# Causal mask of a segment-recurrent attention: a mask product on TensorE replaced by a minimum on VectorE, with a new order of operations

## The chip, the cores and the metric

The kernel runs on one core of a Trainium2 chip. The core has five engines that the text names as the profile does: PE (TensorE, matrix products into the accumulation banks; PEld are its weight loads), DVE (VectorE), ACT (ScalarE), POOL (GpSimd) and SP (SyncE, which issues most DMAs). Each engine works through its own instruction list in the written order and waits on semaphores of the others. The metric is device time in microseconds of one launch, lower is better. A profile is one further execution, taken by the hardware profiler.

## The reference, cut to what matters

Two attention branches read the same `x` (2048 rows of 512, bfloat16) and are mixed by a gate per row. Branch A is the one that the change touches. It goes through the rows in 64 segments of 32 rows, with 8 memory rows in front of each:

```python
mask = (idx[:, None] < M) | (idx[:, None] >= idx[None, :])   # M = 8, idx = 0..39
for s in range(n_seg):                                        # 64 segments
    h = jnp.concatenate([mem, xs], axis=1)                    # 8 memory rows + 32 rows
    q, k, v = h @ Wq, h @ Wk, h @ Wv                          # 32 heads of 128
    scores = where(mask, q k^T * scale, -1e9)
    o = softmax(scores) v, then Wo
    mem = o[:, :M]                                            # the next segment needs this
    outs.append(o[:, M:])
return g * a + (1 - g) * b
```

So segment s + 1 cannot project its memory rows before segment s has been through all of it. Memory rows see every column; the others see columns up to their own. Branch B is a causal softmax attention in four blocks of 512 rows with a small memory between the blocks; its parts hang less on each other.

## The kernel before, in words

**Work.** A class `Prog` records every operation with its engine, its reads and its writes. `ORDER`, a packed text at the head of the file, then says for each engine in which order the operations stand; semaphores are put in from the reads and writes. Where an operation may run on either of two engines (the copies out of the accumulation banks on ACT or DVE, some small products on DVE or POOL), `ORDER` decides that too. So the engines are in order, and what stands behind a waiting instruction waits with it.

**A segment** (`p_seg`) treats 24 of its rows and the 8 memory rows as keys and columns of `hT`; the last 8 rows of every segment don't depend on the memory as keys, and their projections come from batches for four segments at once (`p_rest`, tiles `xr`, `rem_k`, `rem_q`, `rem_v`). The steps are, for each half of the heads (r = 0 and 1, 16 heads each):

- projections of K and Q (line 1422, `Wk_sb,hT` and `Wq_sb,hT`, 16 matrix products each of 512 columns, or two times 16 of 256 columns for the last Q), copied to `st` by ACT or DVE (line 1002) and transposed on DVE into `KT_sb` and `QT_sb` (line 1497);
- the mask product (operation `H`, `f_hide`, in the profile under the helper's line 1029 with the tiles `hide_sb,neg_sb`): four matrix products of 160 columns that put -1e9 where a score is to be hidden and 0 elsewhere;
- the scores (operation `S`, lines 1512 and 1516), added onto that;
- the exponential on ACT (line 1521) into `PT_sb`, 56 columns for each of four head groups;
- the sums over keys by a product with ones (operation `U`, line 1536), the logarithm of the sums and the exponential of its negative on ACT (lines 1540 and 1542: the reciprocal), and the products with it on DVE and POOL (lines 1544 and 1546);
- the values (operations `PV` and `PW`, lines 1577 and 1586), copied to `OT_sb`.

After both halves comes the output projection (line 1314, `Wo_sb,OT_sb`, 64 matrix products), a transposition on DVE (line 1332), the exchange of two halves (line 1335) and the sum that writes the memory columns of the next `hT` (line 1337). The V projections (line 1422, `Wv_sb,hT`), the batches of `p_rest`, the last rows' output projections (`Wo_sb,OTr_sb`) and all of branch B stand in between as other work.

The lines of the operations that the change touches:

Of the kernel before, what the change touches and what calls it, by code (L numbers as in the profile page):

```python
# [15 lines left out]
    "c-nPZ2|yIp8~@(U?#`aDpc0BE%HfgsomYk;kY(l-rCDN{VwqNIYMyCore%1Rnn!rynSz9h;(Z%lq-kEEsR;@!3(U@&|9i8?yczhf!tTy|^S$r*eZTK}Pd5Y_F;`It7Qt!M>jdXFZ"  # L16
    "o}-UlLQEyp%Znl@BL;{n;K2$&H>mTz4SFmT->}>Uj3k}Ax1#@|F)jy%a)CuJat}R+mVI0VSn<{jtTiAHr)-JHnVW?7+7^4Mjwxk0EEq7O){4P{F=1({YSvLVSQH!nLG4W_PiTg50"
    "2~?Cjevt%qpGqX9JTf2%N|n43{DSW=?CJH`$aW^l;(b7AT27at_>WV<G2E+e=NC_xT4})(%_O;1cK|@!%sMuR5FrosV`z$GZL-ngj8W-QHDeyQR&AmT>-AJX~r9w&EP<vf>k13>}"
    "YuMGWGzU!~8%&JQ-1f(c4LLI~N5IeQV0#?OF2!QE<RZ?L2efGsfP4iSf(uCn}cIN$12`{P+6F9gn+{LDZu1y+Cn%`e0KXaOQp5~=dwr?T)a2rjn0i#RdRP*D_60^lgLUW?-3T5AD"
    "jybi^^oj}%>U%zo>Jb8OZ<N}L1(=#JDDoS_`pkgh2B0%=U>r|~rbo`cqusO2TW~0a<WCe1=<RUh>xlYGAT@awnt*sMpDAF5er(SIgaCr*VEC!Gp!1GiZ{)5^AJm?7j_+?@1XVC66"  # L20
    "fK}v0dtnjOMt8&ES#TM#+-5CV24f)gF^mT=dd2_h7_tMPi`R}>Q*C+|IKc{F8M+b*CahBw{|@l86F&Jw<gJA$VEhbw5jb2flMdk9=>lxN@wK9KSIXHo05@sWTy_w|B0V@xG|X$k!"
    "5Qc(z>l4d0gO{L*8zySK|+AI=Yc|?i|A>-rv~5b&x$60G`~bF5g;`*UeUgp8#$P~WuO<H3;HrU6qp@?poi!G*1ZFJdo>Z@TR5FXf;4NkN4_;Q_>=tEN6g`@fLb1bpaQZOiBXA>+V"
    "H_fUo0j7tZRV`qWIE%l9QVe4i}WBen=dJJ$-3R$`vD)ECd(}i!6v}wbKMbU|KIybFj0I<yVs21`WWjcz74CIxX<zN6}V_>`=sknfI7Lom-iDQqlY4j3tj35S_u#NIL8@#(|@(^gD"
    "q0MO1`W<fvwgK|q|<WpWYQIAZErNVb+NA!hN)%6Z)m)oCLd#K2<P`G#<>Spirme1+>R!DTrEufjoS2e3LBmW(FSix)!Cv_)X{<k$nW+{BAwE4V<Gi@XNJ6qu-J|I%D~`W1pX(dr6"
    "(Zsdy$M1J#|UcaIjK_A87OP!BGmm~3{MiDW2`b1JS#zG4zYL8z&jn!$w&VgMtAR!PCfvr_vXm#I&D5^58Xr!WX?sD?;Wsu1EGvETU^t@Rm^QJ;WnomV`C2^nywC;mQ$Yfy?Ur|D_"
    "+x^7LIRr4fPb(%|7#Kycye@;J*805BKVblW2D^Y*GHwNd0uQboqwdro;&<wLP(!K-hDODb5;6!@=<%CuNDROMkMxyQ!@7G&;`g2uwoqyYIK2&-U4g}V{#iBP3SzT(=$yDIx0r};d"
    "Nfrr`}5L`NyOOQqQPFs*-F9YE_D=Av!#v~1t^1;Pt@?xMDN{1dK?MP(&QfgfDlfp4L48({ACl!_Z={bdSQl?kBP9gHeF!YDiZ}!fSaJ`F@)>OoG{{7l9QCr;5++xqT}nYJ(f%ef~"
    "c~)u+~#VO0>bU0*1m<2xW-kOk04bH`epzFFYc_HvHD-Ka11iv=>z?H<I=tQX?Qxb~61n`atq8hKl#IxN?r?i*2q4HEG5LAY^gk%flVv+w|Ack1N&eV+-P*$I%~$fqC(V=2F6+_tK"
    "`$8cX!18sAl7csb{#;Jk*=Paxt!Za1~P%cZhXN^zu1U15uA4^8D0gNtMmY~^4ON{QNWB&IM|jnZ6*Xhn-kCz4tQhr7rk=C+VQPuR<@C=B(ynW-%49~@;K9!UNyT@S$JF#tytozt5"
    "C5q%x@h_(LpPy`V@*Acw6w7TY-iq_!{C<tnj^Sg(%r<~diL6o##{=@EL37^jN263L+F9ox%n6xg^Gt&DDu=FUTEBz%LVBu$V;StF#Po6I_Sl#@!P^<e$H^}ZKKyE(N>>^7aeuavs"  # L30
    "k{{#SP{$7ig0u5Y#H#>}Wt<&{zDiRhT?0mtAHBEmPeKPL;WPxrHfu(gCf6ag`T(LL?1@J_fS6ROGaBXcH@L-8_<H^ipOtaX;r-0nFvbWeghvU(DST1;KExcXR$dh9w3HG@%d90<&"
    "ZW<b$c$)3=>3m_l&*Y%8{2^}?JvWB^OX~U;fkSdIUfR$4m;v2B`Bx%y#9>54MH3xB7MT$<H0T`m}T6&coXW6Tz;aqV#X!tpSC9S7t)}gBN}W{riGy>zgB*<TzR7uy-}OUuQyyO)-"
    "siOn$h@AL#ivGJ0EhjT1YoyYvW@MFLY>wp|);&Ib8AT;<D}gmu1TFWeRi2Xv>GoU=hpKt%IM&zyT+LjSMg{%J4pXZF;3H(_mrLFQqV+Mk!eItZb1NzWE}MK`K&_YyvM`A%AvKzYV"
    "6M0H<G6fTl+~AFZw|9zwo$KKdS=2?!i51O%%Fm0IS_mN~K|<SP-X20y3A9NgotFGgo9z#&ED)b^)HyWPWZdZABn)#r-7Kv>_;>|+c47YjIdg`vPoNGMcK=SH8l(t6$@=uwE7Cp>8"
    "J4G5f9fY3Gsdp_1c|2}SxF2o#+IoO!z`7&Dd$OV5rg4fas^_$65>v`>`tO75lLm)1OSd4-&iXHX_h^bH?qYv@SS-tpTj8@=i{0!Fx@dx;B>^y*$&Ibf2aaey?M-8ZvZ+2K906G;w"
    "WHuyZ#$|TBj5~wi3Yz~Vw*NjLKy;YPcpls)v}Wj_Jww``O8;rn?AhSbTfj}M4%p7)QNd<#1yT{P@4!jC%?t&m@28UsI&1?}pF;uNPRSB&F4OJ+^+iK~Symw&j*0|(Ke%>FY#=)BN"
    "0spfp&%?Kz=B6z9)ysf+03461+@^^-o}?i&M^U}c-C+77cFah+fy~TfT9r3H41Qh_k%GH?u0wY8qIIZc3Da0hh!jwt)LdMEzr%qwFd=0Yf$sPLpEI?83~L)1Ja1Ir4Am7O(Z5i7H"
    "sQrz;oYifr9W2n9Nw<l2@YM>RO+vTNqYiL!3<xQL)MTck{vq0&;jvo<Gh^0@8rGT41v2z;L1?*n+3d2;pr7mOweE(dIlIws*&e8XG)n-JF5!io%L><BK7Hv&ktcHjy~mb#d?~jV!"
    "hHj}G5V!QGw)64V9AOABTQzYPI(_@{P9>#MSPW`ymLx8jZ+ez)#j6d+sV=8A(zM$#eqPWZlF9-{?1D%y77{uvWcu*Wk2=1nIHIxroS<Q3gq^AiCitVL6|%S*}&loDNz?@|#Ovrg7"
    "tVs-B{y-BQ})dBi8M82qy(AlnBfoa~TlvstPHxaIbt8p>sJ>DE0b{9e41Ft?THB#-==UG!__3IXK+mmE1QP(Vx{pH-D1WKNm@Fcc2U4-G+QC{ppooCOXH7RU|H$SZ$i`v6)H=-7b"  # L40
    "VYu9TE#oa2e;Z&jsaRW&V{)EovUA||DA8f|LP&=Ln{Y%?&x_<KQD;2W0SBf{m_LaM<h6(5pzs2C2JQ12AqAhbglp-*#);na7n|lyhXr4N4HEHLgWwPD#SSD!HVDR{8{Tu6y*US{T"
    "kwLx);kMarJ>-i{{Z3k#8<PtesK_jfMBE~8$sYcJX(AOU-e^=7McSr$ZHXiS};|I!wb9Pdqj^{>_L5m!wW)1Ls6Lb%H0O&)dMxW-~+*eaNMm3PL2ezgRlUCx~tOTlSM@YAZOAy(+"
    "z^dU-Z??&t7;^!!dagxF)QSuheG>mt@P{{&6k&yP1Anj1uhzysfLXqOsecGwI$Kd#-IvuRHeD@OQnTYhdUyFp@WD)?z{RsFYnxlhNo;lcTNY6C1fJ96$HrHx0|rXq`8t&3>?OYX?"
    "<)v4CH<205=bz9qa^@ie%`w2z&>@rdipAA1>}Y<sNaEnKu|7!KOjkIQ_`aOA`+2z);0%UvJ+8~U&==D!`yqx>Z^gP?-f8^WGLRxBJYiwogJsIWS%SPX(jZ_m)f`L?y(R5c1SxjAF"
    "em3A((TYd)g<DKgO4K}3}ggy+(tB<TAIIyr_ivBEgIMqG7`|tZV8~Nw9D~(7yxX?66;Pox<=z@QIw_#p%1sPj_sQLbL4t`I7jDfJ_Z8&ptNO=pV37awgBQ*N`wG}1~GOjj$hb(@x"
    "$L$wMgZv5_=6w(3`p8ws<7k`RxA?wD+K|&itkvnWA-iuO*&o67enCHF?^!q*%58Z1OtOy7fU|ejn+1Dczju7PY33VEZbgYEJY~*<8jquiU0IN@um83IuqEc;fV9~lbWf`VqK&)Wm"
    "@~|T_g<pj2L%-x!C1<pcE^eLHa#6l!5o)a|8f)IZe0_I*B$SjT>DXlfrGOT6Un`zj+c|WkZq92lVI-X?FktNt3M_87S^#sd~n-hT=Dtxk;_RShz%LNchAa`N5NyA-ii47OK#CbjE"
    "4Rc^wok2GbtuAle8~)ID=&y0*D2I*$(JxvpV<c=QYQ<4LMV6CJM-jDZSOqaN@tjO^FD;T4yG=+*XVo7hj_Jsxx99+TA-Oq<sF@XIoYD%>=UYnHDCl>A8##$O79wD6U_|6HbL$lY)"
    "S+undQd2qO6_jog+ZyNH7X6Sog?C!dI=2Pkl1KD5Wikt?t`I+f<+{ntJs*MsKn${?xgeze#OBK1p$Y84|uV=_#Ue~D%h>OFlQU_Ey*&XzU+-hz>jXE^Uix-A&Fr=~#1b49^Jh$ZB"
    "Kj3fJ@+zZ6kmx~U+wPRvFpyWP1U{ofqun~D`&-jOX!<z3!3Fz{j=<AVtzRDBfac~gS&et0pZaR>l_PUYFY0QSs{%Y$07~WG4=}=;-Nj8(vvuTS#-)wPnpQZHPiQHq>dsF0v*66`$"  # L50
    "81>sk!f}o4=bK;Vih@c{_TEkYK(+s%9xsqdfk*h>+efG&@G)9Cb3sM|ByQTA7#@gc%@N^J;~-8?#`T0Lo%$1vTLwZs&QgZSQ{RpY`Y6R#VSYEYZqj_YZflnF*tB*qiP>jM1v76Lx"
    "E0K`Z#2O-8y9gratC7)%HIur>2P_oH=a5yYQkI;n?VCiEI!?xR{q1S1Ny>01x@Z%OiXc3SV99w9Ex1ok02W&F&$f`osM!Wg6KOHpZqKX7=?>w%-6eOCfSAKok<17?w1P)`fgwR$O"
    "OidduJj~x$o(-yYpW(YG}hZ1SQBsGeG8i?(EC<)WH$&EZ#B^F0=#KIRvhU+i`mD-JdS&pVnU<ev@8sI$U`0Hu3RNGCp5lw!B>5^PH|(F4V5>B1tBS4tKQUb5GF4xmyy)en0m6C^L"
# [83 lines left out]
class Slot(Res):  # L137
# [9 lines left out]
    @property  # L147
    def b(self):
        return self.banks[0]
# [1498 lines left out]
```

## Time and profile before

| | |
|---|---|
| time, median of 3 runs | 824.7 us (823.15 to 830.68) |
| the profiled execution: its own time, its span | 824.12 us, 822.2 us |
| PE busy | 795.5 us (97%) |
| PEld busy | 506.2 us (62%) |
| DVE busy | 642.5 us (78%) |
| ACT busy | 523.4 us (64%) |
| POOL busy | 259.7 us (32%) |
| mask products (line 1029, `hide_sb,neg_sb`) | 512, 31.5 us busy, 233 ns mean |
| exponentials (line 1521) | 128, 45.5 us busy, 356 ns mean |
| products with the reciprocal (line 1544) | 128, 44.2 us busy, 345 ns mean |

Span is the time from the first to the last instruction, and the launch's own time is 1.9 us more. Busy times are shares of the span on each engine. Matrix products overlap each other in PE, so the mean duration of one is longer than the time between the starts of two; the busy time is that of their union.

### The profile page before, as it was taken

How to read it: one execution, taken by the hardware profiler on the slowest of the kernel's cores; microseconds unless marked ns; L12 is line 12 of the kernel's file. 1: busy time of each engine (PE TensorE's matmuls, PEld its weight loads, DVE VectorE, ACT ScalarE, POOL GpSimd, SP SyncE). 2: the span in 40 equal slices, each digit the busy share in tenths (PEclk: the TensorE clock that was granted, in tenths of full speed). 3: DMA queues.
4: the chain of work that ended last, by engine and by line, in shares of the span. 5: the costliest groups of instructions: out<-in, count | busy, mean ns of one | idle time of the engine just before them, and what ended most of it. 6: DMA issues, size and time to landing. Idle time of an engine off the chain costs nothing.

```text
span 822.2 us, 51771 instructions
## 1 busy us (share of the span) xinstructions
PE 795.5 (97%) x23607; PEld 506.2 (62%) x23607; DVE 642.5 (78%) x1681; ACT 523.4 (64%) x1198; POOL 259.7 (32%) x564
## 2 busy tenths in 40 slices
PE   9999999999999999999999999999999999999987
PEld 4456666656666566666656665656765666666655
DVE  4878888778879777777877887787876788787886
ACT  4666656776656656767667666577666656766662
POOL 4543221233223332422422322333323223332440
PEclk9999999999999999999999999999999999999999
DMA  9982202121210111121011111100111010010001
GB/s 337 414 243 58 51 9 43 35 51 27 47 25 21 45 27 39 32 46 33 16 37 47 37 24 44 30 24 19 40 47 29 22 30 22 16 25 22 22 21 36
DMA packets 71696, 45.14 MB, mean 55 GB/s; under 512 B 50046, under 2 KB 69942, under 8 KB 69942
## 3 DMA queue, kind: packets, MB, share of 16 engines
q1 hardware_dynamic: 70422, 40.92, 17.6%
q8 instruction: 185, 3.03, 1.6%
q10 hardware_dynamic: 1056, 0.92, 0.4%
q14 instruction: 33, 0.27, 0.1%
HBM read 30.33 MB, written 8.87 MB: 48 GB/s over the span
## 4 chain that ended last, share of the span: by engine, by line
PE 84%; DVE 7%; ACT 3%; DMA 2%; issue 2%; POOL 0%; SPq 0%; DVEq 0%; POOLq 0%
PE pb L1422 45%; PE pb L1314 17%; PE pb L1029 6%; PE pb L1146 4%; PE pb L1577 2%; PE pb L1187 2%; PE pb L1031 2%; PE pb L1512 2%; PE pb L1536 1%; PE pb L790 1%; DMA out_dram<-stg 1%; PE pb L1586 1%; DVE V_sb L1002 1%; PE pb L1235 1%; DVE OT_sb L1002 1%
## 5 line engine op out<-in xcount | busy, mean ns | idle before, releaser
L1164 ACT ACTIVATE PTB<-pb 128x640 bf16<-128x640 f32 x240 | 158.4, 704 | 41.8 <-PE pb L1146 30.5
L1002 ACT ACTIVATE st<-pb 128x512 bf16<-128x512 f32 (+2 forms) x232 | 113.1, 499 | 106.8 <-PE pb L1422 80.7
L1422 PE MATMUL pb<-Wv_sb,hT 128*32 128x512 bf16 x2048 | 153.4, 380 | 0.0
L1422 PE MATMUL pb<-Wq_sb,hT 128*32 128x256 bf16 (+1 forms) x3072 | 140.0, 308 | 0.5 <-DVE hT L1337 0.3
L1314 PE MATMUL pb<-Wo_sb,OT_sb 128*32 128x256 bf16 x4096 | 131.4, 273 | 5.1 <-issue 3.8
L1422 PE MATMUL pb<-Wk_sb,hT 128*32 128x512 bf16 x2048 | 132.3, 379 | 1.0 <-issue 0.6
L1314 PEld LDWEIGHTS pb<-Wo_sb,OT_sb 128*32 128x32 bf16 x4096 | 102.1, 96 | 16.1 <-issue 4.2
L1170 POOL TENSOR_SCALAR_AFFINE_SELECT PTB<-PTB 128x512 bf16<-128x512 bf16 x120 | 78.1, 651 | 90.9 <-ACT PTB L1164 84.3
L1422 PEld LDWEIGHTS pb<-Wq_sb,hT 128*32 128x32 bf16 x3072 | 80.9, 97 | 41.7 <-DVE hT L1337 3.8
L1546 POOL TENSOR_TENSOR PT_sb<-PT_sb,rc_sb 128x64 bf16<-128x64 bf16 x81 | 29.6, 365 | 188.4 <-ACT rc_sb L1542 179.3
L1422 PEld LDWEIGHTS pb<-Wk_sb,hT 128*32 128x32 bf16 x2048 | 54.6, 97 | 48.9 <-DVE ao L1345 2.2
L1002 ACT ACTIVATE OT_sb<-pb 128x320 bf16<-128x320 f32 (+1 forms) x139 | 57.4, 429 | 34.4 <-PE pb L1586 32.2
L1002 DVE CAST st<-pb 128x512 bf16<-128x512 f32 (+1 forms) x123 | 67.2, 549 | 15.4 <-PE pb L1422 12.8
L1002 DVE CAST OT_sb<-pb 128x320 bf16<-128x320 f32 (+2 forms) x121 | 56.5, 475 | 20.6 <-PE pb L1586 18.2
L1002 DVE CAST V_sb<-pb 128x512 bf16<-128x512 f32 x90 | 61.5, 683 | 9.9 <-PE pb L1422 8.8
L1497 DVE STREAM_TRANSPOSE QT_sb<-st 128x128 f32<-128x128 f32 (+1 forms) x192 | 61.8, 334 | 7.8 <-ACT st L1002 5.7
L1540 ACT ACTIVATE rc_sb<-pb 128x160 f32<-128x160 f32 x128 | 38.9, 304 | 43.8 <-PE pb L1536 37.0
L1332 DVE STREAM_TRANSPOSE pb<-pb 128x256 f32<-128x256 f32 x63 | 29.3, 465 | 42.4 <-PE pb L1314 42.2
L1422 PEld LDWEIGHTS pb<-Wv_sb,hT 128*32 128x32 bf16 x2048 | 49.5, 97 | 19.2 <-ACT st L1002 0.7
L1521 ACT ACTIVATE PT_sb<-pb 128x224 bf16<-128x224 f32 x128 | 45.5, 356 | 23.3 <-PE pb L1516 19.4
L1497 DVE STREAM_TRANSPOSE KT_sb<-st 128x256 f32<-128x256 f32 x128 | 54.5, 426 | 7.0 <-ACT st L1002 5.5
L1544 DVE TENSOR_TENSOR PT_sb<-PT_sb,rc_sb 128x160 bf16<-128x160 bf16 x128 | 44.2, 345 | 9.0 <-ACT rc_sb L1542 7.4
(200 smaller groups left out, 1461.3 us busy)
## 6 DMA issues: line engine op xcount, KB each, us to landing
Wv_sb<-in_A_Wv_dram SPq DMA_DIRECT2D x4, 1024.0 KB, 10.1
Wk_sb<-in_A_Wk_dram SPq DMA_DIRECT2D x4, 1024.0 KB, 20.5
Wq_sb<-in_A_Wq_dram SPq DMA_DIRECT2D x4, 1024.0 KB, 27.3
Wo_sb<-in_A_Wo_dram SPq DMA_DIRECT2D x4, 1024.0 KB, 20.7
rest_v<-stg SPq DMA_DIRECT2D x112, 32.0 KB
rem_v<-rest_v SPq DMA_DIRECT2D x28, 128.0 KB, 2.4
a_rows<-ao SPq DMA_DIRECT2D x63, 32.0 KB
stg<-a_rows SPq DMA_DIRECT2D x15, 128.0 KB
```

Source lines behind the costliest of these rows:

```text
L1002: self.P.op(("act", "dve"), (lambda a: a.activation(dst, src(), ACT.Copy), lambda d: d.tensor_copy(dst, src())), reads=reads, writes=write ...
L1029: ins = pe.matmul(out[32 * c:32 * c + 32], lhsT[:, 32 * c:32 * c + 32], rhs, start=start, stop=stop, tile_position=(0, 32 * c), **kw)
L1146: ins = pe.matmul(pb[slot.banks[i]][:, base + a - lo:base + b - lo], KT[r0:r1, 128 * kc:128 * kc + 128], Q[r0:r1, t0 + a:t0 + b], start=Tr ...
L1164: P.op("act", (lambda dst=dst, src=src: lambda a: a.activation(dst, src(), ACT.Exp, scale=0.25))(), reads=[pair], writes=["%s%d_%d" % (nam ...
L1170: P.op("gp", (lambda pt=pt, ii=ii: (lambda g: g.affine_select(pt, pt, ([[0, len(ii)]] if len(ii) > 1 else []) + [[1, 128]], ALU.is_ge, 0.0 ...
L1314: ins = pe.matmul(pb[so.b][p0:p0 + 32, 0:256], tok(r, g, l), half(h, d, q), start=(r == 0 and g == 0 and l < 2), stop=(r == 1 and g == 3 a ...
L1422: ins = pe.matmul(self.pb[sl.b][32 * g:32 * g + 32, 0:hi - lo], x[:, c, 0:32], cols, start=(c == 0), stop=(c == C - 1), tile_position=(0, ...
L1497: op("dve", (lambda dst=dst, src=src: lambda d: d.transpose(dst, src))(), reads=["st%d%s" % (i, tag)], writes=["%sT%d%s" % (kind, r, tag)] ...
L1521: op("act", lambda a: a.activation(PT[:, r, :], pb[rb.b][:, 0:224], ACT.Exp, scale=SCALE), reads=[rb], writes=["PT%d" % r, "PT%dr" % r], n ...
L1540: op("act", lambda a: a.activation(rc[:, r, :], pb[rb.b][:, 0:160], ACT.Ln), reads=[rb], writes=[rr], name="ln%d_%d" % (s, r), cost=t_act( ...
L1544: op("dve", lambda d: d.tensor_tensor(mine[r], mine[r], by_head(rc[:, r, :]), ALU.mult), reads=[rp, rr], writes=[rp], name="nrm%d_%d" % (s ...
L1546: op(("dve", "gp"), tuple((lambda e: e.tensor_tensor(rest[r], rest[r], late(rc[:, r, :]), ALU.mult)) for _ in range(2)), reads=[rp + "r", rr],
```

## The change

The mask product `H` is taken out of each half segment, and the first score product of each group now starts the bank afresh (`start=(l == 0)`). The exponential then works on scores that are not masked. Behind it DVE takes, in place, the minimum of the first 40 columns of each head group of `PT_sb` and a table: zero where the score is to be hidden, 3e38 elsewhere. The sums and the products read `PT_sb` behind that minimum. The table is made once: the old mask product is done a single time (`keep`), and a DVE instruction turns what it gives into zeros and 3e38 and writes it over `hide_sb`. `ORDER` is another text throughout.

```diff
 ORDER = (
-    "c-nPZ2|yIp8~@(U?#`aDpc0BE%HfgsomYk;kY(l-...
+    "c-nPZ2VfLM7k;yQm)&b=1f&NDgx-tvDumudT2Pww...
 )
...
+        sm = P.slot("F")
+        op("pe", lambda pe, m: self.mm(pe, m, pb[sm.b][:, 0:160], self.neg[:, :], self.hide[:, :], True, True), reads=["neg", "hide"], writes=[sm],
+           name="keep", cost=0.08, prio=-0.98, mode=FLEX)
+        op("dve", lambda d: d.tensor_scalar(self.hide[:, :], pb[sm.b][:, 0:160], -0.5, 3e38, op0=ALU.is_ge, op1=ALU.mult), reads=[sm], writes=["hide"],
+           name="keepev", cost=0.3, prio=-0.98)
...
         def p_s(r, i, prio):
             rb = bank()
 
-            def f_hide(pe, m):
-                return self.mm(pe, m, by_head(pb[rb.b][:, 0:224])[:, :, 0:40], self.neg[:, :], self.hide[:, :].rearrange("p (h q) -> p h q", h=4), True, True, skip_group_check=True)
-            op("pe", f_hide, reads=["neg", "hide", "st%d" % i], writes=[rb], name="H%d_%d" % (s, r), cost=0.072, prio=prio, mode=FLEX)
-
             def f_sc(pe):
...
-                                        start=False, stop=True, tile_position=(0, 32 * g), skip_group_check=True)
+                                        start=(l == 0), stop=True, tile_position=(0, 32 * g), skip_group_check=True)
...
             op("act", lambda a: a.activation(PT[:, r, :], pb[rb.b][:, 0:224], ACT.Exp, scale=SCALE), reads=[rb], writes=["PT%d" % r, "PT%dr" % r],
                name="exp%d_%d" % (s, r), cost=t_act(224), prio=prio)
+            op("dve", lambda d: d.tensor_tensor(by_head(PT[:, r, :])[:, :, 0:40], by_head(PT[:, r, :])[:, :, 0:40], by_head(self.hide[:, :]), ALU.min),
+               reads=["hide"], writes=["PT%d" % r, "PT%dr" % r], name="cut%d_%d" % (s, r), cost=0.3, prio=prio)
```

Counted from the two orders: PE issues 505 matrix products fewer (the 512 mask products go; the table's product and other splits of the same work add 7). DVE gets the 128 minima and the table's instruction. Of the copies out of the banks that either engine can make, 39 more stand on ACT than before, counted with the exchanges of line 1335; of the copies of projected K, V and Q alone it is 21, 18 and 24. PE changes between its ways of dividing its array 376 times, before 380 times. The table is made before the first segment's scores.

More of the change, by code (lines that the diff above doesn't have):

```diff
@@ L20 @@
[L20 to L43, printed above, removed]
@@ L76 @@
[L76 to L79 removed]
+    "c-nPZ2VfLM7k;yQm)&b=1f&NDgx-tvDumudT2Pwwj{F296zK>8p-77;9YI7CLI^!-q=q68>7b|-NlY%>C3m+o|IA+5axrk1yV*ByUin@ds9f>|hr{`NKn8ea#0$9j3%O4m2G1%EJ"
@@ L80 @@
+    "J|ox^o^gFnYKX<8oSi@<ct8x0gO0_eq|W+x&Y}apZ*?Mm5;o4uaeg&26xfnh7{;4Q1)s-6c7>Jm6ZP$RW%~(=4RhFqzVsp-5{EVGw=@=Ky;T#N&^>A7X8O%CqddSl@OyF%hyKOH{"
+    "Kx3VfL9*as%)2UF~?u*o~OPC>cFRu)+>eOCsem+j}lO05M3Yp#cWUlE(q#dM}UYZXYl2KX~}>-03d%S3Qn1IjGm@ab6%$ZXR_bKqa69X~5zfrh%losn>+2S12zC0wqErLK?UDViD"
+    "<Xll~8w$TxZ"
 )
```

100 lines of the change are left out of this document (60 added, 40 removed).

## The prediction

> **What bounds the kernel now.** I read the page's busy times first, then the chain that ended last, then one segment in order of time, then who waited for whom on PE's weight loads.
>
> ```profile
> span 822.2 us, 51771 instructions
> PE 795.5 (97%) x23607; PEld 506.2 (62%) x23607; DVE 642.5 (78%) x1681; ACT 523.4 (64%) x1198; POOL 259.7 (32%) x564
> ...
> PE 84%; DVE 7%; ACT 3%; DMA 2%; issue 2%; POOL 0%; SPq 0%; DVEq 0%; POOLq 0%
> ```
>
> By these rows PE is nearly always at work, and any matrix product taken away would be time won. The order of time of one segment, from the memory columns of one to those of the next, tells another story.
>
> ```profile
> 400.37 0.19 DVE L1337 TENSOR_TENSOR hT<-pb,other_sb 128x32 bf16<-128x32 f32 x1
> 400.87 1.04 PE L1422 MATMUL pb<-Wk_sb,hT 128*32 128x512 bf16 x16
> 401.73 1.04 PE L1422 MATMUL pb<-Wq_sb,hT 128*32 128x512 bf16 x16
> 402.14 1.28 ACT L1002 ACTIVATE st<-pb 128x512 bf16<-128x512 f32 x2
> ...
> 403.69 0.40 DVE L1497 STREAM_TRANSPOSE QT_sb<-st 128x256 f32<-128x256 f32 x1
> ...
> 403.68 0.24 PE L1029 MATMUL pb<-hide_sb,neg_sb 128*32 128x160 bf16 x4
> 403.75 0.61 PE L1422 MATMUL pb<-Wq_sb,hT 128*32 128x256 bf16 x16
> 404.40 0.27 PE L1512 MATMUL pb<-QT_sb,KT_sb 128*32 128x40 bf16 x16
> 404.82 0.36 ACT L1521 ACTIVATE PT_sb<-pb 128x224 bf16<-128x224 f32 x1 [1.40 <-PE pb L1516]
> 405.40 0.27 PE L1536 MATMUL pb<-PT_sb,ones_sb 128*32 128x160 bf16 x8
> 405.54 0.49 DVE L1497 STREAM_TRANSPOSE QT_sb<-st 128x128 f32<-128x128 f32 x2
> 406.20 0.25 PE L1029 MATMUL pb<-hide_sb,neg_sb 128*32 128x160 bf16 x4
> 406.27 0.28 PE L1512 MATMUL pb<-QT_sb,KT_sb 128*32 128x40 bf16 x16
> 406.69 0.36 ACT L1521 ACTIVATE PT_sb<-pb 128x224 bf16<-128x224 f32 x1 [0.27 <-PE pb L1516]
> 407.27 0.29 PE L1536 MATMUL pb<-PT_sb,ones_sb 128*32 128x160 bf16 x8
> 407.95 0.34 ACT L1542 ACTIVATE rc_sb<-rc_sb 128x160 f32<-128x160 f32 x1
> 408.32 0.33 DVE L1544 TENSOR_TENSOR PT_sb<-PT_sb,rc_sb 128x160 bf16<-128x160 bf16 x1
> 409.39 0.27 PE L1577 MATMUL pb<-PT_sb,V_sb 32*128 32x40 bf16 x16
> 409.62 1.93 PE L1314 MATMUL pb<-Wo_sb,OT_sb 128*32 128x256 bf16 x64
> 411.61 0.47 DVE L1332 STREAM_TRANSPOSE pb<-pb 128x256 f32<-128x256 f32 x1 [0.82 <-PE pb L1314]
> 412.55 0.19 DVE L1337 TENSOR_TENSOR hT<-pb,other_sb 128x32 bf16<-128x32 f32 x1 [0.26 <-ACT other_sb L1335]
> ```
>
> From 400.37 to 412.55 are 12.18 us, and 64 such turns are 780 us of the 822.2. So the time is that of this ring of steps, and PE's other work is laid into it in a written order. The reader is to see two kinds of links. In the tight ones the next engine starts as soon as it can: the product with the reciprocal starts at 408.32, 0.03 us behind the reciprocal's end (407.95 and 0.34), the turn at 411.61 right behind the output projection. In the slack ones PE is late, because other work stands in front: the scores start at 404.40, 0.31 behind the last transposition (403.69 and 0.40); the sums start at 405.40 and 407.27, both 0.22 behind the exponential's end; the values start at 409.39, 0.74 behind the product with the reciprocal. The whole run agrees:
>
> ```profile
> PEld pb L1536 <- ACT PT_sb L1521: 7.3, 30, 0.4
> PEld pb L1422 <- DVE hT L1337: 5.9, 18, 0.9
> PEld pb L1577 <- DVE PT_sb L1544: 5.2, 14, 0.9
> ```
>
> Only 30 of the 128 sums had PE waiting for the exponential, so in most segments PE was the later one there; 18 of 63 segments had it idle at the start for the memory columns. Neither PE nor the ring binds alone: a link that gets longer is hidden where PE is late, and PE's time that is saved counts only where PE is late.
>
> The Trainium skill, Perfetto Trace Analysis, section Identifying the Most-Contended Engine, says that the share of matmul busy time is no good measure of how near PE is to its limit, since matmuls are pipelined. The trace agrees: 16 products of K last 1.04 us, and the next 16 start 0.86 us later. By the page's 97% alone the sum would be the first term below and nothing else.
>
> **Part one, the mask products leave PE.** The rows have products behind a mask product 0.07 us after it (403.68 to 403.75, 406.20 to 406.27), though its busy time reads 0.24. 128 times 0.07 are 9.0 us of PE's turns: an upper bound, as it counts only where PE is the late one. In the segment above that holds at the first scores, while before the second PE waited for the transposition anyway. I take half, -4.5 us. The lower end is nothing.
>
> **Part two, the minimum enters the ring.** No row shows a minimum of two bfloat16 tiles. The nearest are on the same tile:
>
> ```profile
> L1544 DVE TENSOR_TENSOR PT_sb<-PT_sb,rc_sb x128: 263/324/829, 51.7 to 814.7; 128x160 bf16<-128x160 bf16 x128
> L1546 DVE TENSOR_TENSOR PT_sb<-PT_sb,rc_sb x47: 202/218/655, 68.4 to 813.7; 128x64 bf16<-128x64 bf16 x47
> ...
> L1544 DVE TENSOR_TENSOR PT_sb<-PT_sb,rc_sb 128x160 bf16<-128x160 bf16 x128 | 44.2, 345 | 9.0 <-ACT rc_sb L1542 7.4
> ```
>
> Behind the colon stand the shortest, median and longest in ns. The first has the same 160 elements but a float32 second operand, the second has 64 elements. The minimum has 160 elements, all in two bytes, so I bound it by 0.22 and 0.34 us and take 0.29, nearer to the row with its size. The Trainium skill, VectorE: DVE Perf Modes, section The perf-mode tier table, gives `tensor_tensor` on bfloat16 in SBUF twice the float32 rate; by that an estimate is 0.24 us, and the ring's bill below would be 3 us smaller. With the 0.03 of the tight hop the link from exponential to sums grows by 0.32. The second half is the one on the ring: 64 times 0.32 are 20.5 us. Against it stands the cover: PE came 0.22 behind the exponential, 0.19 more than a tight hop; 64 times 0.19 are 12.2 us. What is left is +8.3 us. Without any cover it is +20.5, with 0.34 for the minimum +23.7.
>
> The new order moves cover to this place. Between the second half's scores and sums stand 28 matrix products per segment, before 18; from the first projection to the first scores they fall from 84 to 74, and between the second sums and the values from 50 to 47. This hides the new link on PE, but the work is taken from links that were waited for too, so I count it as neither gain nor loss.
>
> **Part three, DVE's and ACT's queues.** The engine is in order: behind a first-half minimum stands, in 38 of 64 segments, a transposition of the second half, which would otherwise have run while the exponential did; behind a second-half minimum stands in 30 segments the first half's product with the reciprocal. The scores of the second half wait for the former. I put 38 times 0.08 (a quarter of the minimum) on the ring, 3.0 us, and 0.05 for every second-half minimum that finds DVE in a longer instruction, 3.2 us: an estimate, between nothing and, with the whole 0.29 in 38 segments, 11 us. The Trainium skill, SBUF — State Buffer, section SBUF: two separate sides, says that a DVE instruction with two SBUF inputs and a GpSimd instruction that reads SBUF exclude each other. The minimum is of that kind, like line 1544, whose longest took 0.829 against a median of 0.324; its mean of 345 ns in the grouped rows makes this 0.02 us each, under 2 us in all if every one were on the ring.
>
> DVE's total does not grow, by the copies that the new order hands to ACT:
>
> ```profile
> L1002 DVE CAST V_sb<-pb 128x512 bf16<-128x512 f32 x90 | 61.5, 683 | 9.9 <-PE pb L1422 8.8
> L1002 DVE CAST st<-pb 128x512 bf16<-128x512 f32 x66 | 44.5, 674 | 9.6 <-PE pb L1422 8.9
> L1002 DVE CAST st<-pb 128x256 bf16<-128x256 f32 x57 | 22.9, 403 | 5.8 <-PE pb L1422 3.9 <-PE pb L1029 1.1
> L1002 ACT ACTIVATE st<-pb 128x512 bf16<-128x512 f32 x126 | 75.2, 598 | 71.0 <-PE pb L1422 69.6 <-PE pb L1029 0.5
> ```
>
> Minima: 128 times 0.29, 37 us. Gone to ACT: 18 of V (12.3 us), 24 whole ones of K and Q (16.2) and 21 half ones (8.5), together 37 us. On ACT they are some 34 us, which lifts it from 523 to about 557, 68% of the span. ACT waited 69.6 us for PE before such copies, so I cost this at nothing; if that cover is gone, an exponential waits behind a copy of 0.6 us. The table's product, its DVE instruction and the four-product start are paid once, in the first 50 us.
>
> **Sum.** -4.5 + 8.3 + 3.0 + 3.2 = +10.0 us on the profiled execution's 824.1 us: 834.1, so 834. The median of the runs, 824.7, lies 0.6 above that execution, and the measurement of this kernel tells about 1% from no change, 8.2 us.
>
> **Rivals.** *PE binds after all.* If the moved work covers the minimum in every segment, all 9.0 us of PE's turns are won: 815.1, faster. It decides where the new cover of 10 more products outlasts the link's 0.32 us, at the sums. For it: 16 products take 0.86 us from start to start, so 10 take 0.54 us. Against it: the projections' link, which lost 10 products, now has PE idle until the transposition's end.
>
> *It cancels.* The minimum is covered, but the ring sets the time, and PE merely waits where it worked: 820 to 830, about 825. For it: DVE's unchanged total, and the idle waits in the rows above. This is also the case in which the change does not do what it says: PE's turns go, and the time does not.
>
> *The full bill.* DVE's order puts each minimum late and the cover is spent elsewhere: +20.5 and +6.2, with little won back, 846 to 850. For it: the ring has tight links on both sides of PE. Against it: the 98 sums at which PE did not wait.
>
> **How the numbers follow.** My forecast, slower by 830 to 842 with 834 likeliest, gets 0.40; the full bill 0.10; cancelling 0.27; PE binding 0.23. The forecast's lower end lies within 1%, which takes 0.03 of it. So: slower by over 1% (past 833) 0.47, within 1% 0.30, faster by over 1% (under 816.5) 0.23. The range is 812 to 848: below, 815.1 and 3 us for a shorter ring by the other order, which no row bounds; above, the dearer minimum without cover, +23.7, which makes 847.8.
>
> **What would show each step.** The minimum's line on DVE: 128 of 0.22 to 0.34 us. DVE near 642 us busy, ACT near 557. PE's busy time and its mask group gone, but PE's waits for DVE before the sums longer than the 7.3 us for ACT above. The stretch from one memory sum to the next grown from 12.2 us by about 0.15. I am wrong if the sums hardly wait and the stretch is shorter by 0.14, twice 0.07: then PE's turns were the bound.

## The result, and the profile after

The changed kernel takes 829.4 us (826.96 to 831.71, 20 runs), the kernel before takes 824.75 us on the same chips (820.24 to 830.68, 20 runs). The ratio is 1.0056 with a 95% interval of 1.0040 to 1.0073: the change makes the kernel slower by 4.6 us. The forecast was +10, so the sign was right and the size less than half.

The head of the profile's page and the chain that ended last, of the changed kernel:

```profile
span 825.9 us, 50882 instructions
PE 792.4 (96%) x23092; PEld 494.3 (60%) x23102; DVE 652.3 (79%) x1765; ACT 547.5 (66%) x1237; POOL 257.3 (31%) x570
...
PE 79%; DVE 9%; ACT 4%; DMA 3%; issue 3%; SPq 2%; POOL 0%; DVEq 0%; POOLq 0%; ACTq 0%
```

The mask products have gone from PE, DVE has 10 us more and ACT 24. PE's share of the chain falls from 84% to 79%, and DVE's rises from 7% to 9%: a little more of the end is now set by DVE. The minimum's own line (shortest, median and longest in ns, then who waited for it, in us and times):

```profile
L1524 DVE TENSOR_TENSOR PT_sb<-PT_sb,hide_sb x128: 193/243/726, 49.4 to 817.1; 128x160 bf16<-128x160 bf16 x128
...
  PEld pb L1539: 15.8, 54
```

and the same operation in the groups, with its mean:

```profile
L1524 DVE TENSOR_TENSOR PT_sb<-PT_sb,hide_sb 128x160 bf16<-128x160 bf16 x128 | 34.7, 271 | 10.7 <-ACT PT_sb L1522 8.7
```

PE waited for a minimum at 54 of 128 sums, where before it waited for the exponential at 30. In order of time, one segment's exponentials (line 1522), minima (1524) and sums (1539) look like this:

```profile
406.75 0.36 ACT L1522 ACTIVATE PT_sb<-pb 128x224 bf16<-128x224 f32 x1
...
407.14 0.72 DVE L1524 TENSOR_TENSOR PT_sb<-PT_sb,hide_sb 128x160 bf16<-128x160 bf16 x1 [0.18 <-ACT PT_sb L1522]
...
407.92 0.29 PE L1539 MATMUL pb<-PT_sb,ones_sb 128*32 128x160 bf16 x8
...
408.67 0.36 ACT L1522 ACTIVATE PT_sb<-pb 128x224 bf16<-128x224 f32 x1
...
409.19 0.24 DVE L1524 TENSOR_TENSOR PT_sb<-PT_sb,hide_sb 128x160 bf16<-128x160 bf16 x1
...
409.47 0.40 PE L1427 MATMUL pb<-Wq_sb,xr 128*32 128x512 bf16 x4
...
409.68 0.28 PE L1539 MATMUL pb<-PT_sb,ones_sb 128*32 128x160 bf16 x8
```

The second half is the more frequent case (74 of 128): the minimum ends at 409.43, PE then still has a batch projection (`Wq_sb,xr`, from 409.47) in front of the sums and starts them 0.25 us after the minimum. The minimum is hidden. In the first half of this segment the minimum took 0.72 us, and PE waited for it.

To see where the time went I took from the trace the start of every step of the ring and averaged the distances over segments 1 to 62 (us; S scores, U sums, PV values, the figure behind them the half of the heads; "plain" has neither mask product nor minimum, so that the mask is left out, and the three columns in the middle belong to runs told below). The first projection is the first product of K or Q that starts behind the memory sum; the end of the output projection is taken as the start of its last product:

| link | before | old order, plain | old order, minimum | new order, plain | after |
|---|---|---|---|---|---|
| first projection to S0 | 3.69 | 3.62 | 3.62 | 3.52 | 3.53 |
| S0 to S1 | 1.58 | 1.55 | 1.76 | 1.58 | 1.60 |
| S1 to U1 | 1.02 | 1.02 | 1.27 | 1.33 | 1.38 |
| U1 to PV1 | 1.97 | 2.00 | 1.93 | 1.88 | 1.87 |
| PV1 to the end of the output projection | 2.00 | 1.96 | 1.95 | 1.94 | 1.93 |
| from there to the next first projection | 1.80 | 1.81 | 1.85 | 1.84 | 1.79 |
| the whole turn | 12.06 | 11.97 | 12.37 | 12.10 | 12.10 |

Between before and after, the link from S1 to U1 is 0.36 us longer; the first link is 0.16 shorter, that from U1 to PV1 0.10 and the one behind it 0.07. That is a small difference of large changes, so the question was which part of the edit makes which. Each column is of one execution, and that of the old order with minimum took 845.8 us, 3.8 above the median of its kernel, which is 0.06 us of a turn.

### The profile page after: what moved, and what is told of

It is laid out like the page before. It is cut to its first block, busy times and chain, and to the rows that moved or that the text cites. A ratio compares the mean times of both kernels' runs of the same rounds, so it can differ in the third digit from the quotient of the medians.

```text
span 825.9 us, 50882 instructions
## 1 busy us (share of the span) xinstructions
PE 792.4 (96%) x23092; PEld 494.3 (60%) x23102; DVE 652.3 (79%) x1765; ACT 547.5 (66%) x1237; POOL 257.3 (31%) x570
## 3 DMA queue, kind: packets, MB, share of 16 engines
q1 hardware_dynamic: 70422, 40.92, 17.2%
## 4 chain that ended last, share of the span: by engine, by line
PE 79%; DVE 9%; ACT 4%; DMA 3%; issue 3%; SPq 2%; POOL 0%; DVEq 0%; POOLq 0%; ACTq 0%
PE pb L1427 42%; PE pb L1319 16%; PE pb L1034 5%; PE pb L1151 3%; PE pb L1580 2%; PE pb L1513 2%; PE pb L1192 2%; DMA st<-in_gate_w_dram 2%; PE pb L1539 2%; PE pb L1036 1%; DVE st L1007 1%; SPq L1396 1%; PE pb L1589 1%; DMA rest_v<-stg 1%; DVE V_sb L1007 1%
## 5 line engine op out<-in xcount | busy, mean ns | idle before, releaser
L1007 ACT ACTIVATE st<-pb 128x512 bf16<-128x512 f32 (+2 forms) x274 | 133.5, 501 | 91.6 <-PE pb L1427 74.1
L1427 PE MATMUL pb<-Wv_sb,hT 128*32 128x512 bf16 x2048 | 155.5, 380 | 0.9 <-issue 0.9
L1427 PE MATMUL pb<-Wq_sb,hT 128*32 128x256 bf16 (+1 forms) x3072 | 142.7, 308 | 0.8 <-DVE hT L1342 0.4
L1319 PE MATMUL pb<-Wo_sb,OT_sb 128*32 128x256 bf16 x4096 | 129.3, 273 | 2.2 <-issue 1.8
L1427 PE MATMUL pb<-Wk_sb,hT 128*32 128x512 bf16 x2048 | 129.7, 379 | 0.8 <-DVE ao L1350 0.4
L1427 PEld LDWEIGHTS pb<-Wq_sb,hT 128*32 128x32 bf16 x3072 | 79.1, 97 | 43.3 <-DVE hT L1342 3.0
L1007 ACT ACTIVATE OT_sb<-pb 128x320 bf16<-128x320 f32 (+1 forms) x133 | 55.5, 428 | 37.7 <-PE pb L1589 36.8
L1007 DVE CAST OT_sb<-pb 128x320 bf16<-128x320 f32 (+2 forms) x127 | 59.7, 476 | 23.6 <-PE pb L1589 22.2
L1007 DVE CAST st<-pb 128x256 bf16<-128x256 f32 (+1 forms) x78 | 43.0, 552 | 14.0 <-PE pb L1427 13.1
L1007 DVE CAST V_sb<-pb 128x512 bf16<-128x512 f32 x72 | 49.0, 682 | 4.1 <-PE pb L1427 3.0
## 6 DMA issues: line engine op xcount, KB each, us to landing
Wv_sb<-in_A_Wv_dram SPq DMA_DIRECT2D x4, 1024.0 KB, 10.4
```

Source lines behind the costliest of these rows:

```text
L1007: self.P.op(("act", "dve"), (lambda a: a.activation(dst, src(), ACT.Copy), lambda d: d.tensor_copy(dst, src())), reads=reads, writes=write ...
L1319: ins = pe.matmul(pb[so.b][p0:p0 + 32, 0:256], tok(r, g, l), half(h, d, q), start=(r == 0 and g == 0 and l < 2), stop=(r == 1 and g == 3 a ...
L1427: ins = pe.matmul(self.pb[sl.b][32 * g:32 * g + 32, 0:hi - lo], x[:, c, 0:32], cols, start=(c == 0), stop=(c == C - 1), tile_position=(0, ...
```

## The experiments

Each run is meant to change one thing against before or after. The order of operations was taken apart from the work: the same packed text for the order of before or of after, with only the operations added or left out that the work needs. The minimum's table has a tile of its own, `table_sb`, in them. Ratios are against the kernel before on the same chip, and I give the difference as the ratio times 824.75 us. The median of the kernel before was 821.0 to 826.0 us in the rounds told here, so runs of different rounds compare by their ratios and not by their times.

### The parts in the old order

`old_plain` takes the mask products out and puts nothing in their place. `old_both` keeps them and has the minimum too. `old_min` is the changed kernel's work in the order of before, each minimum placed in DVE's list where its exponential ends. `old_mask2` has every mask product twice.

```diff
# old_min, against before
-            op("pe", f_hide, ... name="H%d_%d" % (s, r), ...)
-                                        start=False, stop=True, ...
+                                        start=(l == 0), stop=True, ...
+            op("dve", lambda d: d.tensor_tensor(by_head(PT[:, r, :])[:, :, 0:40], by_head(PT[:, r, :])[:, :, 0:40], by_head(self.table[:, :]), ALU.min), ...)
# old_plain: without the last line; old_both: only the last line; old_mask2: only a second op like f_hide (start=False)
```

> The order of before, with the 128 mask products taken out and no minimum put in: the mask is left out altogether, so only the time is read. Theory (ring and PE share the path, half of PE's turns count): 128 x 0.07 us x 1/2 = 4.5 us less than before, about 820. Rival, PE binds: the whole 9.0 us less, about 816. Rival, PE only waits where it worked: no change, 824 to 826.

> The order of before with its mask products, and the minimum added behind each exponential, where it changes nothing in the result: the minimum's price alone, without cover moved to it. Theory: 64 x 0.32 less 64 x 0.19 of cover, 8.3 us, and 3 to 6 us for DVE's queue, so 11 to 15 us more than before, 836 to 840. Rival, PE binds and hides the minimum: under 3 us more. Rival, full bill: 20 to 27 us more, 845 to 852.

> The changed kernel in the order of before: mask products out, minimum in, each minimum where DVE came to it in the trace of before. Theory, by the sum of the prediction, in which the order counts for nothing: 10 us more than before, 835. Rival, the new order is what kept the change cheap: clearly slower than the changed kernel, by 5 us or more. Rival, the new order itself costs: faster than the changed kernel, under 826.

> The kernel before with each mask product done twice (the second adds onto the first; hidden scores are -2e9): the price of PE's turns by adding instead of taking. Theory: half of 9.0 us, 4 to 5 us more than before. Rival, PE binds: 9 us more. Rival, PE's turns there are free: no change. If taking away wins nothing and adding costs, PE's turns lie just under the cover.

Measured: `old_plain` 823.8 us, ratio 0.9978 (0.9953 to 1.0003); `old_both` 845.9, 1.0248 (1.0217 to 1.0279); `old_min` 846.9, 1.0252 (1.0219 to 1.0286); `old_mask2` 841.8, 1.0198 (1.0167 to 1.0229).

So the minimum costs some 20 us in the old order, more than the theory had: `old_both` lies in its rival's range, the full bill. Beside the minimum the mask product costs nothing that shows (`old_both` and `old_min` differ by 0.0004). `old_mask2`, 16.3 us above before, is beyond all that was expected of it. But `old_plain` had a trap in it. Its link from U1 to PV1 was 2.14 us against 1.97 before (0.17 us more; the expectation of `p_old_plain` has 0.22), though nothing in that link was edited. The program gives each operation one of eight accumulation banks by modelled times, and with other work in the list it chose other banks for more than half of the 1287 uses in each of the four runs. They therefore change two things at once. In what follows the banks are written into the kernel, before's for the old order and after's for the new. `old_both` and `old_mask2` were not done again so: whether the mask product is free beside the minimum, and what a second one costs, stays open.

### The same with the banks held

> The order of before without mask products and without minimum (the mask is left out), now with every accumulation bank written into the kernel as before had it: without that, 857 of 1287 bank uses had moved, and the steps from the sums to the values were 0.22 us longer per segment though nothing was changed there. Theory, the moved banks ate a gain of PE's turns: 5 to 9 us less than before, 816 to 820. Rival, PE's turns are free: 823 to 826, like the run with moved banks.

> The changed kernel in the order and with the banks of before. Theory, the minimum lengthens the ring by 0.25 us per segment there and nothing hides it: 838 to 846, so that the new order is worth 9 to 16 us. Rival, the moved banks made the 20 us of the unpinned run, and the order counts for little: 829 to 835.

> The changed kernel's order and banks without the minimum and without mask products (the mask is left out). Theory, the new order has work standing where the minimum was to be hidden, so taking it away wins little: 1 to 5 us less than the changed kernel, 824 to 828. Rival, the minimum still costs on the ring there: 10 us or more less, under 819.

> The changed kernel's order and banks, with a mask product in front of each half's scores as before and no minimum: the work of before in the new order. Theory, the new order is not better in itself, it only puts cover at the new link: 828 to 836, not faster than before. Rival, the new order is the better one for any work: under 820.

`p_new_plain` is the changed kernel in its own order without the minima, `p_new_mask` has a mask product ahead of each score group instead, as before. All four came out within their theory's range or at its edge.

| run | order | mask product | minimum | us | ratio (95%) | us against before |
|---|---|---|---|---|---|---|
| `p_old_plain` | before | no | no | 819.8 | 0.9946 (0.9924 to 0.9967) | -4.5 |
| before | before | yes | no | 824.75 | 1 | 0 |
| `p_old_min` | before | no | yes | 842.0 | 1.0211 (1.0182 to 1.0240) | +17.4 |
| `p_new_plain` | after | no | no | 828.1 | 1.0044 (1.0025 to 1.0063) | +3.6 |
| `p_new_mask` | after | yes | no | 829.6 | 1.0054 (1.0029 to 1.0080) | +4.5 |
| after | after | no | yes | 829.4 | 1.0056 (1.0040 to 1.0073) | +4.6 |

This table is the answer to the sum (a single entry has an interval of some 2 us to either side, so that a price of 1.0 is not to be told from nothing). The mask product costs 4.5 us in the old order. The minimum costs 21.9 us there, and 1.0 in the new order. The new order by itself, with the same work, costs 8.1 us (`p_old_plain` to `p_new_plain`). -4.5, +21.9 and -12.8 for the new order with the minimum in place make +4.6.

Where the 21.9 come from is in the waits of PE's weight loads before the sums (us in all, times, longest). In `p_old_plain` they wait for the exponential:

```profile
PEld pb L1563 <- ACT PT_sb L1548: 9.6, 37, 0.4
```

In `p_old_min` they wait for the minimum:

```profile
PEld pb L1574 <- DVE PT_sb L1559: 66.4, 125, 1.0
```

37 sums waited, now 125 of 128 do. One second half of `p_old_min` in order of time shows how long the new link is:

```profile
415.47 0.36 ACT L1557 ACTIVATE PT_sb<-pb 128x224 bf16<-128x224 f32 x1 [0.16 <-PE pb L1552]
415.86 0.32 DVE L1582 TENSOR_TENSOR PT_sb<-PT_sb,rc_sb 128x160 bf16<-128x160 bf16 x1
...
416.09 0.24 DVE L1559 TENSOR_TENSOR PT_sb<-PT_sb,table_sb 128x160 bf16<-128x160 bf16 x1
416.38 0.13 PEld L1574 LDWEIGHTS pb<-PT_sb,ones_sb 128*32 128x32 bf16 x8 [0.62 <-DVE PT_sb L1559]
416.39 0.29 PE L1574 MATMUL pb<-PT_sb,ones_sb 128*32 128x160 bf16 x8
```

The exponential ends at 415.83, the first half's product with the reciprocal stands in front of the minimum in DVE's list, and PE has been idle for 0.62 us when the minimum is done. On the mean of the segments, second half, there are 0.16 us from the exponential's end to the minimum's start, 0.25 of minimum and 0.07 to the sums: 0.48, where `p_old_plain` has 0.23 from exponential to sums.

### Which half is on the ring, and what of it is DVE's queue

`p_old_min_h0` and `p_old_min_h1` have the minimum in one half only, and the other half is left without a mask. `p_old_scr` has all 128 at their places, but into a scratch tile, so that no sum waits for them; it leaves the mask out.

```diff
# p_old_min_h0 / h1
+            if r in (0,):     # (1,)
                 op("dve", lambda d: d.tensor_tensor(by_head(PT[:, r, :])[:, :, 0:40], ..., ALU.min), ...)
# p_old_scr
-            op("dve", lambda d: d.tensor_tensor(by_head(PT[:, r, :])[:, :, 0:40], by_head(PT[:, r, :])[:, :, 0:40], by_head(self.table[:, :]), ALU.min),
+            op("dve", lambda d: d.tensor_tensor(by_head(self.table[:, :]), by_head(PT[:, r, :])[:, :, 0:40], by_head(self.hide[:, :]), ALU.min),
```

> Order and banks of before, no mask products, the minimum only for the first half of the heads (the mask of the second half is left out). Without any minimum this order took 819.8 us, with both 842.0. Theory A, read from the links of the ring: both halves sit on it, the first by 0.2 us per segment between the two score groups, so +10 to +13 us, 830 to 833 us. Rival B, the step of the prediction: only the second half is on the ring and the first costs some 3 us, so 823 us.

> The same with the minimum only for the second half (the mask of the first half is left out). Theory A: the link from the second scores to the second sums grows by 0.15 to 0.25 us, +9 to +13 us, 829 to 833 us. Rival B: nearly the whole bill of 22 us is here, 838 us or more.

> The same with all 128 minima at their places in VectorE's list, reading the exponential's tile, but writing a scratch tile that nobody reads (the mask is left out): sums and products no longer wait for them. What is left is what the minima do in VectorE's queue: their 0.24 us and their wait for the exponential with a transposition behind them. If the first half's cost is that queue, about half of the 22 us stays, 829 to 832 us. If it is the link on TensorE (the first sums stand in front of the second scores there), little stays, 820 to 823 us.

Measured: first half alone 830.1 us, 1.0072 (1.0045 to 1.0099), which is 10.4 over `p_old_plain`; second half alone 834.9, 1.0130 (1.0094 to 1.0167), 15.2 over it; scratch 829.2, 1.0057 (1.0038 to 1.0077), 9.1 over it. The prices of the halves add to 25.6, both at once cost 21.9.

The links say why. With the first half's minimum alone only the link from S0 to S1 grows, from 1.55 to 1.77; with the second half's alone only that from S1 to U1, from 1.02 to 1.27. The waits before the sums, with the minimum in the first half alone:

```profile
PEld pb L1574 <- DVE PT_sb L1559: 32.6, 62, 1.0
```

and in the second half alone:

```profile
PEld pb L1574 <- DVE PT_sb L1559: 34.2, 62, 1.1
```

The first half is on the ring through PE's list: in the order of before its sums stand ahead of the second half's scores in 60 of 64 segments, and PE, waiting at the sums, starts the scores later. Theory A was right in kind on both halves, for the second a little low (9 to 13 us).

Of the scratch run I expected either half of the bill or next to nothing, by what the first half's cost would be. It kept 9.1 us, the number of the first case, but its links show a third thing: S0 to S1 grows by only 0.05 us and U1 to PV1 by 0.05, and the products with the reciprocal start 0.08 to 0.13 us later behind their reciprocal than in `p_old_plain`. So DVE's queue has a price, but it is spread over what else stands in that queue. It can't be taken as a part of the 21.9, because where sums wait for the minimum, DVE's later steps have that time too.

### Moving cover in the old order

If the bill is only missing cover at the sums, a simple move of PE's other work should pay it. Four orders tried that, with before's banks; only in the two swapped ones could 257 of the 1288 uses not be kept and were chosen anew. The operations of segment 20 on PE, `p_old_min` first:

```diff
-S20_0 bnz6 v20_0 v20_0_1 wor4_1 U20_0 v20_0_2 ... S20_1 wor4_3 PV20_0 PW20_0 v20_1_3 U20_1 wor4_4 ...
# p_old_fill: one piece from behind the sums to ahead of them (40 first, 59 second sums)
+S20_0 bnz6 v20_0 v20_0_1 wor4_1 v20_0_2 U20_0 ... S20_1 wor4_3 PV20_0 PW20_0 v20_1_3 wor4_4 U20_1 ...
# p_old_swap: first sums behind the second scores, first values behind the second sums
+S20_0 bnz6 v20_0 v20_0_1 wor4_1 v20_0_2 ... S20_1 U20_0 wor4_3 v20_1_3 U20_1 PV20_0 PW20_0 wor4_4 ...
# p_old_s0: q20_1b S20_0 bnz6 ... becomes
+S20_0 q20_1b bnz6 v20_0 v20_0_1 wor4_1 U20_0 v20_0_2 ... S20_1 ...
```

`p_old_swap2` is the swap with the first half's product behind the second minimum on DVE. `p_old_fill_plain` and `p_old_s0_plain` have those orders without the minimum.

> The changed kernel's work in the order of before with one move in each segment: the first half's sums go behind the second half's scores on TensorE, its values behind the second half's sums; on ScalarE the second exponential goes ahead of the first half's logarithm, on VectorE the first minimum behind the last transposition. Theory A: the first half's minimum leaves the ring and the first sums cover 0.2 us of the second's link, so most of the 22 us is hidden, 820 to 827 us. Rival: the first half's reciprocal and products are then the late ones at the values, and the time stays at 838 us or above.

> The changed kernel's work in the order and banks of before, with one kind of move alone: where a piece of TensorE's other work (a quarter of a projection, about 0.22 us) stands behind the sums and ahead of the next step of the ring, it goes in front of the sums: 40 times in the first half, 59 times in the second. Theory A, the minimum's bill is only missing cover at the sums: up to 40 times 0.22 and 59 times 0.22, 22 us, come back, less what the links behind the sums lose; 822 to 830 us instead of 842. Rival B, the links behind the sums are as tight, and the pieces only change where TensorE waits: 836 us or more.

> The same order without the minima (no mask at all): what the 99 moves cost by themselves, against 819.8 us for the order of before without them. Theory A: in the second half there was 0.2 us of slack between product and values, so little, 820 to 824 us. Rival B, cover at the sums has a price like that of the new order, 8 us: 828 us.

> The swapped order, with the first half's product (30 times line nrm, 7 times its second part) put behind the second minimum on VectorE. If the swapped order lost its time because the second minimum stood behind that product, the second sums come 0.5 us earlier and the time falls from 870 to 830 to 842 us. If the cause is elsewhere (the first half's values are late), it stays at 860 us or more.

> The changed kernel's work in the order and banks of before, with the last piece of TensorE's other work ahead of the first scores moved behind them, in 54 segments (29 times the last part of the second half's Q projection, 25 times a piece of V or of branch B). Theory A: the new order found its cover there, where TensorE came 0.15 us later than the transposition allowed; the scores come up to 0.15 us earlier in 54 segments, and 842 falls by 5 to 9 us, to 833 to 837. Rival B: the second scores then wait for the later projection, and the time stays at 840 us or above.

> The same order without the minima (no mask at all), against 819.8 us for the order of before without them. Theory A: without the minimum TensorE has no idle time at the sums to put the moved work into, so nothing is won, 819 to 824 us, and the minimum costs 10 to 16 us in this order instead of 22. Rival B: the moves cost as in the new order, 826 us or more.

| run | minimum | us | ratio (95%) | us against before | the minimum's price in that order |
|---|---|---|---|---|---|
| `p_old_swap` | yes | 869.9 | 1.0563 (1.0533 to 1.0592) | +46.4 | |
| `p_old_swap2` | yes | 850.9 | 1.0364 (1.0345 to 1.0384) | +30.0 | |
| `p_old_fill` | yes | 842.1 | 1.0258 (1.0237 to 1.0280) | +21.3 | 16.7 |
| `p_old_fill_plain` | no | 824.9 | 1.0055 (1.0033 to 1.0077) | +4.5 | |
| `p_old_s0` | yes | 861.2 | 1.0481 (1.0452 to 1.0510) | +39.7 | 24.7 |
| `p_old_s0_plain` | no | 835.8 | 1.0181 (1.0155 to 1.0207) | +14.9 | |

None of them paid, and my theory lost each time; the losses teach more than the first table.

*The fill.* Its 99 moves cost 9.0 us without any minimum. The link from S1 to U1 grows by 0.25 us, a whole piece, while that from U1 to PV1 gets back only 0.12: behind the sums, from the logarithm's start to the end of the product, 1.25 us pass there (1.35 in `p_old_plain`), and the values follow the product by 0.27 us (0.28). So the piece that went from there was not what the values waited for, and ahead of the sums it stands in the way wherever PE was already late. With the minimum the sums still waited, less each:

```profile
PEld pb L1574 <- DVE PT_sb L1559: 44.2, 103, 1.2
```

PE's waits fell from 66 to 44 us, and the ratio did not fall: the second half's sums came 0.58 us behind the exponential instead of 0.48. A shorter wait is not an earlier start.

*The swap.* The first minimum did leave the ring: S0 to S1 is 1.54 us again. But S1 to U1 became 1.81 (1.27 in `p_old_min`). 30 first-half products and 7 of their second parts stood ahead of the second minimum in DVE's list, and they now waited for sums that PE did later. With those behind it (`p_old_swap2`) S1 to U1 fell to 1.41 and the time by 16 us by the ratios, not to the 830 to 842 that I expected: then U1 to PV1 is 2.19 against 1.93. The values still follow their product by 0.31 us (0.30 in `p_old_min`); it is the second half's product that ends 0.25 us later behind its sums, with the first half's product now in front of it. So the rival, late values of the first half, does not show in these means.

*The first scores.* They came earlier, as theory A says, 3.54 instead of 3.62 us behind the first projection in the plain order. Then S0 to S1 grew from 1.55 to 1.92, since in 29 segments the piece moved was the end of the second half's Q projection. Rival B, and more of it than I had put down.

### How long the new order's cover is

`p_new_min2` is the changed kernel with every minimum done twice.

```diff
             op("dve", lambda d: d.tensor_tensor(by_head(PT[:, r, :])[:, :, 0:40], ..., ALU.min), ..., name="cut%d_%d" % (s, r), ...)
+            op("dve", lambda d: d.tensor_tensor(by_head(PT[:, r, :])[:, :, 0:40], ..., ALU.min), ..., name="more%d_%d" % (s, r), ...)
```

> The changed kernel, its order and its banks, with every minimum done twice. If the cover in the new order is just as long as one minimum, the second is on the ring in both halves, 0.24 to 0.27 us each: +15 to +30 us, 845 to 860 us. If TensorE has work to spare at the sums, the second costs a few us as the first did, 830 to 836 us.

Measured: 847.6 us, 1.0265 (1.0220 to 1.0309): the second minimum costs 17.2 us where the first cost 1.0. PE's waits before the sums, which were 15.8 us at 54 sums with one minimum:

```profile
PEld pb L1576 <- DVE PT_sb L1561: 44.8, 98, 1.4
```

The link from S1 to U1 is 1.33 us in the new order without minimum, 1.38 with one and 1.59 with two. Even without a minimum the sums start 0.57 and 0.55 us behind the exponential's end there (first and second half of `p_new_plain`), where in the old order it is 0.25 and 0.23 (`p_old_plain`), and the link with a minimum took 0.47 and 0.48 (`p_old_min`). So the new order puts about as much of PE's work there as one minimum needs, and little more. The mask product finds room there as well (`p_new_mask`, +0.8 us over plain).

## Why the prediction was right or wrong

**Part one** (-4.5): `p_old_plain` gives -4.5, with -6.3 to -2.7 by its interval. The place was right too: the link to the first scores became 0.07 us shorter, the one between the scores by 0.03. That the half came out to the tenth is luck, for it was a guess. And the gain belongs to the old order; in the new one the mask product is worth 0.8 us, inside the interval.

**The minimum's duration** (0.29): median 0.243, mean 0.271. The row with 160 elements was the wrong neighbour, since one operand of line 1544 is float32. The estimate of 0.24 us from the Trainium skill, VectorE: DVE Perf Modes, section The perf-mode tier table, is what the median shows. The mean lies above it because of the long ones below.

**Part two, the ring's second half** (+8.3, and +3.2 for a minimum that finds DVE busy): the minimum alone in that half costs 15.2 us, where the sum had 11.5. The cover was read rightly: without the minimum the sums come 0.23 us behind the exponential on the mean (`p_old_plain`; the sum had 0.22). What failed is the hop. I took 0.03 us on either side of the minimum, from one tight row of a reciprocal and its product, and 0.05 for a busy DVE. On the mean the minimum starts 0.16 us behind the exponential and the sums start 0.07 behind the minimum; with the minimum's own 0.25 the link is 0.48 us, 0.25 more than without, and 64 times 0.25 are 16 us. One segment's best hop is not the hop of 64: the very link I read as 0.03 has a mean of 0.22 us over the segments of before (second half). DVE is often in another instruction when the reciprocal comes: only 15 of the 128 products found it idle.

**Part three, the first half** (+3.0) failed too, by more: 10.4 us. I looked at DVE's list, where a transposition stands behind the minimum, and not at PE's, where the first sums stand ahead of the second scores. "The second half is the one on the ring" was wrong; both are. For DVE's queue beside that (+3.2 for second minima that find it busy) the scratch run gives 9.1 us in all, a price of the queue that is not additive.

**The new order** ("neither gain nor loss") is the step that failed by most, a term put at nothing: with the minimum in place it is worth 12.8 us (`p_old_min` to after), without one it costs 8.1. The 10 more products that the prediction itself counted between the second scores and sums are that cover. So the old order's bill was +17.4, not +10, and the new order took back 12.8 of it. That the forecast's +10 is near +4.6, and on the right side of nothing, is luck: two errors of opposite sign were summed, and with only the one or only the other put right the forecast would have been +17.4 or -2.8.

How it takes it back is shown in part. Against the old order with the minimum, S1 to U1 is 0.11 us longer after, but S0 to S1 is 0.16 shorter, the first link 0.08, and U1 to PV1 and the last link 0.06 each: at the sums PE now does work that it did elsewhere. The largest of these has a cause in PE's list. In 22 of the 64 segments (4 before) the second half's scores now stand ahead of the first half's sums, so that a wait at these sums no longer holds the scores up. There S0 to S1 is 1.06 us with the minimum and without it, against 1.42 in the same segments of `p_old_min`; in the other segments it is 1.88 against 1.93. By an estimate, 21 times 0.36, that is some 7.5 of the 17 us by which these two traces differ. No run makes this move in these segments alone, and `p_old_swap`, which makes it in all 64, loses. Simple moves from behind the sums or ahead of the first scores do not do the same either. Which of the new order's moves are needed, and whether the copies handed to ACT are (after them the minimum starts 0.08 us behind the exponential's end, not 0.16), stays open: the two orders can't be mixed engine by engine, since each list waits for steps that another has in a different place.

**DVE's and ACT's totals** (642 and 557): 652.3 and 547.5. The copies that the sum counted did leave DVE, 36.8 us for minima of 34.7, but it left out what came back: copies of `OT_sb` (58.5 us after, 55.3 before), those of 64 partitions (16.7, before 13.3) and branch B's `QT` and `KT` (8.0, before 6.0). The values waited longer for the product on DVE than before, 9.1 us against 5.2, but they did so without any minimum too (8.9 in `p_new_plain`); what these 10 us cost is not shown.

**The rivals.** 829.4 lies in the range given for *it cancels* (820 to 830), 0.6 us below the forecast's own, and what that rival said is close to what the new order does: minimum and mask product are both covered there, and PE waits where it worked. The *full bill* is the kernel in the old order (842.0; the rival had 846 to 850). *PE binds after all* asked for a minimum that is covered nearly everywhere, and that is so (1.0 us); the 9 us of PE's turns were not won for all that, because they are worth only 0.8 in the order that covers it, and that order costs 8.1.

**What would show.** The minimum's line was right in its median (0.243; the shortest and the longest, 0.193 and 0.726, lie outside 0.22 to 0.34), and the waits before the sums rose as said (15.8 us against 7.3). The stretch of a segment grew by 0.05 us, not 0.15.

None of the orders tried with the full mask is faster than the kernel before. Without any mask, the old order is 4.5 us faster, and that bounds what a cheaper mask could win in it.

## What to carry to other kernels

A step that is put into a loop-carried chain is priced by the mean distance between its neighbours over all turns, hops and queueing included; the tightest row of one turn gives the price too low. Look at the waiting engine's own list as well: what stands behind the wait there (here the second scores behind the first sums) is on the chain too. Cover for a new wait has to come from a link in which that engine was late, and a run with the new order but without the new work tells in one number what the cover costs.

## What the runs showed of the hardware beside that

**Minima beside POOL.** 18 of the minima of the changed kernel took more than 0.33 us. At every one of them a POOL instruction had begun earlier, and the minimum ended 0.09 to 0.11 us behind it. Of the other 110, 28 also have a POOL instruction at work in their first 0.2 us, but in 22 of these it had ended within 0.21 us, and in 5 it began with the minimum or behind it. The longest, seen above at 407.14, has this beside it, in the order of time on POOL:

```profile
407.14 0.64 POOL L1175 TENSOR_SCALAR_AFFINE_SELECT PTB<-PTB 128x512 bf16<-128x512 bf16 x1
```

It ended 0.09 us behind POOL's. That is what the Trainium skill, SBUF — State Buffer, section SBUF: two separate sides, says of a DVE instruction with two SBUF inputs and a GpSimd instruction that reads SBUF: one waits for the other. The trace agrees in these 18, but not everywhere: the minimum at 409.19 took its 0.24 us beside a POOL copy that ran from 409.00 to 409.47. Together the 18 took 3.9 us more of DVE's time than the median of 0.243 us would give.

**The choice of banks.** The same work in the same order took 823.8 us with banks chosen anew and 819.8 with those of before (ratios 0.9978 and 0.9946), with the minimum 846.9 and 842.0 (1.0252 and 1.0211). Each pair differs by 0.3 to 0.4%, in both the intervals still overlap. The longer link, U1 to PV1 with 2.14 against 2.00 us, is in the first pair's traces. Only the banks of the operations were changed, so a part of the program that nobody edits may move the time by more than half of what the change under study does.
